# Moving one pool, one load, three weight jobs and some conversions in a fused attention and two-MLP kernel

## The chip, the cores and the metric

The kernel runs on one core of a Trainium2 chip. The metric is the device time of one execution in microseconds (us), the median of several runs; lower is better. Besides the timed runs there is one profiled execution, and every row shown below is from its trace. Engines are named as in the profile: PE (matmul), PEld (its weight loads), DVE (VectorE), ACT (ScalarE), POOL (GpSimd) and SP (SyncE). POOL and SP do little here but start DMA transfers.

## The reference, cut to what matters

Sparse attention, then two MLPs. The second MLP is where the change lies.

```python
def _moe_ref(x, w_in, w_out, s, b):            # first MLP, 512 -> 2048 -> 512
    r = np.maximum(x @ w_in, 0.0)
    return (s * (r * r) + b) @ w_out

def _moe2_ref(x, w_a, w_b, w_out):             # second MLP, 512 -> 1536 -> 512
    a = x @ w_a
    b = x @ w_b
    return (a * b @ w_out).astype(np.float32)

def reference(**kwargs):
    attn_out = _attn_ref(q, k, v)              # (4, 8, 576, 64), local and strided masks
    x = attn_out.transpose(0, 2, 1, 3).reshape(2304, 512)
    return _moe2_ref(_moe_ref(x, ...), ...)
```

## The kernel before

Every fp32 operand of a matmul is split into a high and a low part (ACT copies the high part, DVE subtracts to get the low one), and each product is three matmul passes.

**First MLP.** Five token blocks (`n` = 0 to 4), 16 feature tiles `f` each: products `h` and `acc`. Attention runs in between. The token blocks' inputs live in two rooms, `xp0` (16 KB per partition) and `xp1` (14 KB); the weights of this part live in `wpb`. In block `n == 4` the room `xp1` holds `spare`, which the weight jobs (below) use. Then these rooms are closed, and the pools `ws`, `tmp`, `rp`, `wx`, `gq`, `rq` are laid into the freed space from its start, in the order in which they are opened. A tile of a new pool waits until every use of the old tile under it has ended.

**Second MLP.** The 2304 tokens are three pairs of blocks of 384 tokens. Each pair has a gate part and an o part.
- The gate part has 12 groups `g`. A group is seven products of 6 matmuls (a 2 by 2 block scheme with seven products in place of eight), in this order: a11, s2, s3, s1, a12, a22 (`t4`, read from `wh`), s4. Text below writes (g, k) for the place right after product k of group g, k = 1 to 7. PSUM banks are reused inside a group: product 5 adds into the bank of product 1, so it waits until ACT has copied product 1 out (`quad` or `u`); product 6 adds into that of product 3; product 3 of the next group waits until DVE has read product 6 (`c`).
- Weights per group: two loads `wf<-w2s` of 512 KB (`s2`, `s3`, started two groups ahead by `fill`) and `wsrc<-w2d` of 256 KB (a11) and 128 KB (a22), started by `source` and then converted by ACT and DVE into `wf` and `wh` by `fill`. `wsrc` is one buffer: its next load is started when the conversion has read it and is needed after product 5 of the following group. All these, the x loads and the `o2w` loads go through the SP queue in order.
- The o part has 42 steps of 6 matmuls, step `i` with a 256 KB weight `o2w` from `w2o` (seven rooms, loaded seven steps ahead). Its right operands `gf` are made from `quad` by `g_form` (ACT, DVE, and in 18 of the 42 cases one more DVE operation on `quad`), 11 steps ahead. `o2_post` takes results out of PSUM.
- The next pair's input: `x2_load` brings `xr` (two blocks of 768 KB) from DRAM, `x2_bias` adds a bias (8 ACT steps in groups 9 to 11), and `x2_forms` has 18 steps (4 of them a DVE operation on `xr`, 14 an ACT copy and a DVE subtraction into `x2w`), done in the o part and the first group of the next pair.

**Weight jobs.** `sums(g, ...)` makes weight combinations once and writes them to DRAM through the POOL queue. Fifteen run in the last block of the first MLP, with `spare` as their room. The last one of these ends as the second MLP begins. The last three, `rest[0]` to `rest[2]`, run in the gate part of pair 0, one step at a time at places listed in `job_at`: one load step (two 256 KB loads `w2r`), 4 DVE sums, 4 ACT copies, 4 DVE subtractions, one step that writes 1792 KB to `w2o` (two pieces of 384 KB and four of 256 KB). Their rooms are `rings` 5, 11, 4 and 10.

**Order.** What runs on an engine is in program order as a scheduler laid it out when the kernel was built: it follows the order of the code where `in_order` holds a step behind the last matmul, and otherwise takes what its model finds ready. DVE and ACT have their own chains (`dve`, `act`) that keep the order of the code.

`o1_last` copies the last block of the first MLP out of PSUM: piece 0 and 3 into `hp` rooms, piece 1 into `hp`, piece 2 into `wx`. It runs between the last matmul of the first MLP and the first conversions of pair 0.

## Time and profile before

| | us |
|---|---|
| timed runs (3) | 907.13, 909.04, 909.31 (median 909.04) |
| profiled execution | 906.53 |
| its span, first to last instruction | 904.8 |
| PE busy in the span | 879.9 (97%) |
| DVE busy | 680.7 (75%) |
| ACT busy | 405.6 (45%) |

The profiled execution took 906.53 us, 1.7 us of them outside its span. It lies 0.6 us under the fastest timed run. PE is the engine that is nearly always busy; what is not PE time is 24.9 us of the span, 5.1 us of it in the first 100 us and 6.1 us in the last 55 us.

### The profile page before, as it was taken

To read this page: it belongs to the slowest core of one execution; us is meant where nothing else is said; L and a number is where in the kernel's file an instruction comes from. 1 tells how busy PE (TensorE), PEld (TensorE's weight loads), DVE (VectorE), ACT (ScalarE), POOL (GpSimd) and SP (SyncE) were. 2 spreads that over 40 slices of the span, in tenths; PEclk is the share of its full clock that TensorE was granted. 3 is DMA by queue.
4 is the path that set the end of the run, shared out by engine and by line. 5 is a ranking of instruction groups with operands and counts; after the bars stand their busy time and mean duration, and the time that the engine had idled before them with its cause. 6 is when DMAs were issued, how large, how long until landed. Compare 5 with 4: busy or idle time off the path is not lost.

```text
span 904.8 us, 17302 instructions
## 1 busy us (share of the span) xinstructions
PE 879.9 (97%) x6274; PEld 805.6 (89%) x6274; DVE 680.7 (75%) x1412; ACT 405.6 (45%) x879; POOL 145.6 (16%) x290
## 2 busy tenths in 40 slices
PE   8999999999999999999997999999999999999997
PEld 6778889999888899988886989999999999999997
DVE  6898995776766687637775888697777796877794
ACT  6777764333433343357563333363323462322251
POOL 6000000000000010014543121005300005200013
PEclk9999999999999999999998999999999999999999
DMA  9965534657766666458999688888667788666486
GB/s 233 289 198 170 158 73 138 156 147 163 199 172 171 163 189 170 125 161 307 365 329 323 205 323 279 301 270 260 182 200 249 251 274 250 187 206 202 163 266 186
DMA packets 184644, 195.70 MB, mean 216 GB/s; under 512 B 108272, under 2 KB 137712, under 8 KB 184560
## 3 DMA queue, kind: packets, MB, share of 16 engines
q1 hardware_dynamic: 166160, 147.07, 55.0%
q0 software_dynamic: 15520, 46.81, 14.8%
q10 hardware_dynamic: 2880, 0.72, 0.5%
q8 instruction: 50, 0.82, 0.4%
q14 instruction: 34, 0.28, 0.1%
HBM read 152.08 MB, written 42.47 MB: 215 GB/s over the span
## 4 chain that ended last, share of the span: by engine, by line
PE 69%; DMA 11%; DVE 6%; ACT 5%; issue 4%; POOL 2%; SPq 2%; POOLq 0%; ACTq 0%; DVEq 0%
PE pp L99 21%; PE h L99 16%; PE acc L99 14%; PE o L99 12%; DMA wsrc<-w2d 4%; DMA w2s<-w2t 2%; PE po L99 2%; DMA o2w<-w2o 1%; DVE quad L618 1%; PE pss L99 1%; DMA w2s<-spare 1%; PE ppt L102 1%; SPq L284 1%; DVE w2t L877 1%; DMA fqk<-in_k_dram 1%
## 5 line engine op out<-in xcount | busy, mean ns | idle before, releaser
L99 PE MATMUL pp<-x2w,wf 128*128 128x384 f32 x1296 | 235.4, 337 | 9.8 <-ACT quad L613 6.3
L99 PEld LDWEIGHTS pp<-x2w,wf 128*128 128x128 f32 x1296 | 227.3, 190 | 12.5 <-ACT quad L613 6.6
L99 PE MATMUL h<-x,w 128*128 128x512 f32 (+1 forms) x960 | 217.3, 374 | 1.1 <-ACT r L795 1.0
L99 PE MATMUL acc<-gt,w 128*128 128x512 f32 (+2 forms) x960 | 210.9, 368 | 1.0 <-ACT w L122 1.0
L99 PEld LDWEIGHTS acc<-gt,w 128*128 128x128 f32 x960 | 175.4, 188 | 24.3 <-ACT w L122 1.4
L99 PEld LDWEIGHTS h<-x,w 128*128 128x128 f32 x960 | 171.7, 188 | 25.7 <-ACT r L795 1.1
L99 PE MATMUL o<-gf,o2w 128*128 128x384 f32 x756 | 133.6, 337 | 2.8 <-issue 1.6
L99 PEld LDWEIGHTS o<-gf,o2w 128*128 128x128 f32 x756 | 131.2, 188 | 4.8 <-issue 4.6
L613 ACT ACTIVATE gf<-quad 128x384 fp32r<-128x384 f32 x126 | 64.1, 522 | 93.3 <-DVE quad L618 69.5
L795 ACT ACTIVATE r<-h 128x512 f32<-128x512 f32 (+1 forms) x80 | 44.2, 553 | 123.9 <-PE h L99 115.1
L1288 POOL DMA_DIRECT2D out_dram<-ot x92 | 51.5, 567 | 280.7 <-DVE ot L1274 274.9
L805 DVE TENSOR_TENSOR r<-r 128x384 f32<-128x384 f32 (+1 forms) x48 | 28.9, 602 | 60.1 <-ACT gt L802 60.0
L618 DVE TENSOR_TENSOR gf<-quad,gf 128x384 fp32r<-128x384 f32 x126 | 67.3, 548 | 7.0 <-ACT gf L613 5.2
L618 DVE TENSOR_TENSOR quad<-pp,quad 128x384 f32<-128x384 f32 x108 | 59.7, 552 | 7.8 <-PE pp L99 6.6
L853 POOL DMA_DIRECT2D w2d<-w2s x36 | 19.7, 546 | 207.8 <-DVE w2s L157 191.0
L613 ACT ACTIVATE wf<-wsrc 128x512 fp32r<-128x512 f32 x36 | 22.6, 628 | 66.2 <-PE pp L99 38.1
L141 ACT ACTIVATE raw<-raw 128x512 f32<-128x512 f32 x66 | 42.6, 669 | 8.1 <-DMA raw<-in_moe_w_a_dram 7.8
L147 DVE SCALAR_TENSOR_TENSOR raw<-raw 128x512 uint32<-128x512 uint32 x66 | 44.3, 687 | 0.7
L99 PE MATMUL pp<-x2w,wh 128*128 128x384 f32 x216 | 44.0, 338 | 0.4 <-DVE quad L618 0.3
L613 ACT ACTIVATE quad<-pp 128x384 f32<-128x384 f32 x36 | 17.5, 487 | 58.4 <-PE pp L99 58.3
L618 DVE TENSOR_TENSOR wf<-wsrc,wf 128x512 fp32r<-128x512 f32 x36 | 24.9, 692 | 21.6 <-ACT wf L613 21.6
L618 DVE TENSOR_TENSOR quad<-quad 128x384 f32<-128x384 f32 x72 | 39.8, 553 | 1.3
(175 smaller groups left out, 1005.1 us busy)
## 6 DMA issues: line engine op xcount, KB each, us to landing
wf<-w2s SPq DMA_DIRECT2D x72, 512.0 KB
o2w<-w2o SPq DMA_DIRECT2D x126, 256.0 KB
raw<-in_moe_w_out_dram SPq DMA_DIRECT2D x28, 512.0 KB
w2d<-w2s POOLq DMA_DIRECT2D x36, 256.0 KB, 3.7
w2r<-w2d POOLq DMA_DIRECT2D x36, 256.0 KB, 4.6
wsrc<-w2d SPq DMA_DIRECT2D x36, 256.0 KB
raw<-in_moe_w_in_dram SPq DMA_DIRECT2D x16, 512.0 KB
raw<-in_moe_w_a_dram SPq DMA_DIRECT2D x12, 512.0 KB
```

What stands on the lines that cost most here:

```text
L99: last_pe[:] = [nc.tensor.matmul(*args, **kwargs).ins]
L102: last_pe[:] = [nc.tensor.transpose(*args).ins]
L141: nc.scalar.activation(out=high.bitcast(F32), in_=high.bitcast(F32), func=AF.Copy, scale=HIGH_SCALE)
L147: nc.vector.scalar_tensor_tensor(out=low, in0=high, scalar=3, in1=low, op0=ALU.logical_shift_left, op1=ALU.bitwise_or)
L284: nc.sync.dma_start(out=room[p0:p0 + STR, first_:first_ + (z - a) // STR], in_=at[e])
L613: i = nc.scalar.activation(**kwargs).ins
L618: i = getattr(nc.vector, method)(**kwargs).ins
L795: relu = nc.scalar.activation(out=r, in_=ph, func=AF.Relu)
L805: nc.vector.tensor_tensor(out=r, in0=r, in1=r, op=ALU.mult)
L853: nc.gpsimd.dma_start(out=w2d[i - 1], in_=w)
L877: vector(out=out_, in0=in0, in1=in1, op=op)
L1288: engines[k % len(engines)].dma_start(out=at.rearrange("(j t) c -> t j c", t=STR), in_=st[i * STR:(i + 1) * STR, j:j + m].rearrange("t j a ...
```

## The change

Four edits, all in the second MLP.
- The pool `wx` is opened first, not fourth, so its one room lies at the start of the freed space (over `xp0`) instead of 28 KB into it (over the end of `xp1`). `ws` and `tmp` shift by 2 KB and stay over `xp0`; the first room of `rp` (ring 3) now touches `xp1`.
- `x2_load` brings one block per call. For the next pair, block one is called after product 2 of group 6, block two after product 2 of group 7; before, both came after product 2 of group 8. The x of pair 0 is loaded as before.
- The places of `rest[1]` and `rest[2]` in `job_at` change; those of `rest[0]` are the same, written differently. `rest[1]`: sums from group 3/4 to 2/3, copies from (5, 1..4) to (4, 3..6), subtractions from (5, 4..7) to (4, 6), (4, 7), (5, 1), (5, 2). `rest[2]`: sums from (7, 1..4) to (5, 4), (6, 5..7), copies from (8, 4..7) to (7, 1..4), subtractions from (9, 1..4) to (7, 5), (7, 7), (8, 5), (8, 6).
- In the o part of pairs 0 and 1 the x forms move from steps 0, 2, 5, 8, ..., 38 (14 calls) to 0, 14, 16, ..., 40 (15 calls), and the two 512 KB fills of group 1 of the next pair from steps 14 and 32 to 35 and 37.

```diff
-    def x2_load(pair):
-        xr = p2.tile([P, 2, KD, TB2], F32, tag="xr", name="xr")
-        for i in range(2):
-            c0 = (2 * pair + i) * TB2
-            queue_sp(out=xr[:, i], in_=o1[:, c0:c0 + TB2].rearrange("(k p) t -> p k t", p=P))
+    def x2_load(pair, xr=None):
+        i = 0 if xr is None else 1
+        xr = p2.tile([P, 2, KD, TB2], F32, tag="xr", name="xr") if xr is None else xr
+        c0 = (2 * pair + i) * TB2
+        queue_sp(out=xr[:, i], in_=o1[:, c0:c0 + TB2].rearrange("(k p) t -> p k t", p=P))
...
-    ws, tmp, rp, wx, gq, rq = (
-        pool(*i) for i in (("ws", 2), ("tmp", 6), ("rp", 5), ("wx", 1), ("gq", NQ2), ("rq", 4))
+    wx, ws, tmp, rp, gq, rq = (
+        pool(*i) for i in (("wx", 1), ("ws", 2), ("tmp", 6), ("rp", 5), ("gq", NQ2), ("rq", 4))
...
-        ((2, 1), (3, 5), (3, 6), (3, 7), (4, 7), *((5, k) for k in (1, 2, 3, 4))),
...
+            (1, 7), (2, 5), (2, 6), (2, 7), (3, 7), (4, 3), (4, 4), (4, 5),
+            (4, 6), (4, 6), (4, 7), (5, 1), (5, 2), (5, 3),
...
-    for k in (4, 5, 6, 7, 7):
-        job_at.setdefault((5, k), []).append(rest[1])
...
-            if pair + 1 < NP2 and g == 8:
+            if pair + 1 < NP2 and g == 6:
                 xr = in_order(x2_load, pair + 1)
+            if pair + 1 < NP2 and g == 7:
+                xr = in_order(x2_load, pair + 1, xr)
                 later_x += [x2_bias(xr), x2_forms(xr)]
...
-                if i == 0 or i % 3 == 2 and i < 40:
+                if i == 0 or i % 2 == 0 and i > 2 * NQ2:
                     next(later_x[1])
-                if i in (14, 32):
-                    in_order(fill, "s2" if i == 14 else "s3", (pair + 1) * NG2 + 1)
+                if i in (len(order2) - NW, len(order2) - NW + 2):
+                    in_order(fill, "s2" if i == len(order2) - NW else "s3", (pair + 1) * NG2 + 1)
```

PE's instructions keep their order throughout. On ACT, at the start of the gate part of pair 0, `spare<-w2t` is the last early weight job's copy, `o1s<-acc,sb` are pieces 0 and 2 of `o1_last`, `wh<-wsrc` is the first a22 conversion and `quad<-pp` the copy of product 1 (and, second, of product 5):

```order
 L888 ACTIVATE spare<-w2t 128x1024
-L613 ACTIVATE o1s<-acc,sb 128x512
-L888 ACTIVATE spare<-w2t 128x1024
-L613 ACTIVATE o1s<-acc,sb 128x512
-L613 ACTIVATE wh<-wsrc 128x256
-L613 ACTIVATE quad<-pp 128x384 x2
+L613 ACTIVATE o1s<-acc,sb 128x512 x2
+L613 ACTIVATE wh<-wsrc 128x256
+L613 ACTIVATE quad<-pp 128x384
+L888 ACTIVATE spare<-w2t 128x1024
+L613 ACTIVATE quad<-pp 128x384
```

The second `o1s`, `wh` and the first `quad` have moved ahead of the last `spare`.

On SP, in groups 6 to 8 of the gate part of pair 0 (pair 1 has the same piece): `xr` is the next pair's x, `w2s_152` to `w2s_154` are the weights of groups 8 to 10, `wsrc` those of a11 (128x512) and a22 (128x256):

```order
 L119 DMA wsrc<-w2d_130 128x256
+L119 DMA xr<-o_107 128x4x384
 L119 DMA wf<-w2s_152 128x1024 x2
 L119 DMA wsrc<-w2d_133 128x512
 L119 DMA wsrc<-w2d_135 128x256
+L119 DMA xr<-o_107 128x4x384
 L119 DMA wf<-w2s_153 128x1024 x2
 L119 DMA wsrc<-w2d_138 128x512
 L119 DMA wsrc<-w2d_136 128x256
-L119 DMA xr<-o_107 128x4x384 x2
 L119 DMA wf<-w2s_154 128x1024 x2
```

One block of x now stands in each of two groups, where two blocks stood in a row.

On DVE, in the o part of pair 0, up to the `o2_post` of the second form (`u2`), before and then now; `gf` and `quad` are the next operands, `xr` and `x2w` the x forms:

```order
L618 TENSOR_TENSOR xr_6666<-xr_6666 128x768
L618 TENSOR_TENSOR gf_6041<-quad_6191,gf_6041 128x384
L618 TENSOR_TENSOR quad_6191<-quad_6191 128x384
L618 TENSOR_TENSOR gf_6042<-quad_6351,gf_6042 128x384
L618 TENSOR_TENSOR quad_6351<-quad_6351 128x384
L618 TENSOR_TENSOR gf_6043<-quad_6505,gf_6043 128x384
L618 TENSOR_TENSOR quad_6505<-quad_6505 128x384
L618 TENSOR_TENSOR x2w_5468<-xr_6666,x2w_5468 128x384
L618 TENSOR_TENSOR gf_6044<-quad_6645,gf_6044 128x384
L618 TENSOR_TENSOR quad_6645<-quad_6645 128x384
L618 TENSOR_TENSOR u2_7026<-o2_6962,u2_7026 128x384
```

```order
L618 TENSOR_TENSOR gf_6041<-quad_6195,gf_6041 128x384
L618 TENSOR_TENSOR quad_6195<-quad_6195 128x384
L618 TENSOR_TENSOR gf_6042<-quad_6352,gf_6042 128x384
L618 TENSOR_TENSOR quad_6352<-quad_6352 128x384
L618 TENSOR_TENSOR gf_6043<-quad_6507,gf_6043 128x384
L618 TENSOR_TENSOR quad_6507<-quad_6507 128x384
L618 TENSOR_TENSOR gf_6044<-quad_6654,gf_6044 128x384
L618 TENSOR_TENSOR quad_6654<-quad_6654 128x384
L618 TENSOR_TENSOR u2_7022<-o2_6962,u2_7022 128x384
L618 TENSOR_TENSOR u2_7024<-o2_6963,u2_7024 128x384
L618 TENSOR_TENSOR gf_6045<-quad_6799,gf_6045 128x384
L618 TENSOR_TENSOR quad_6799<-quad_6799 128x384
```

Four x-form operations (three into `x2w`, one on `xr`) that stood between the start of the o part and `u2` now stand behind it; one on `xr` (of step 0) is still ahead of it.

## Rows read from the trace of the kernel before

**Rows 1.** What PE waited for: us in total, times, longest.
```profile
PE pp L99 <- ACT quad L613: 6.3, 1, 6.3
...
PE o L99 <- issue: 1.6, 2, 0.9
```

**Rows 2.** By stage: length, engines' busy us, PEclk, DMA share, GB/s; gate, o alternate.
```profile
587.27:632.97 45.70, 44.34 (x254) 43.76 (x253) 39.73 (x79) 20.92 (x45) 13.09 (x24) 1.00 0.85 268
632.97:721.20 88.23, 87.96 (x505) 87.14 (x504) 67.11 (x132) 29.28 (x64) 8.93 (x17) 1.00 0.67 217
721.20:767.30 46.10, 44.76 (x254) 43.84 (x254) 39.73 (x79) 21.77 (x47) 11.34 (x21) 1.00 0.85 271
767.30:854.70 87.40, 87.40 (x506) 87.40 (x506) 66.15 (x130) 24.47 (x54) 6.66 (x12) 1.00 0.59 192
...
484.63:587.27 102.64, 92.72 (x505) 90.03 (x504) 77.08 (x157) 35.53 (x76) 17.42 (x25) 0.95 0.80 280
```

**Rows 3.** PE's timeline, gate part of pair 0: start, us, instructions [idle before, releaser].
```profile
484.63 4.35 PE L99 MATMUL pp<-x2w,wf 128*128 128x384 f32 x24
495.31 2.29 PE L99 MATMUL pp<-x2w,wf 128*128 128x384 f32 x6 [6.33 <-ACT quad L613]
...
498.87 6.42 PE L99 MATMUL pp<-x2w,wf 128*128 128x384 f32 x36
...
520.76 3.29 PE L99 MATMUL pp<-x2w,wf 128*128 128x384 f32 x18
...
530.60 6.53 PE L99 MATMUL pp<-x2w,wf 128*128 128x384 f32 x36 [0.20 <-DVE quad L618]
...
568.02 3.29 PE L99 MATMUL pp<-x2w,wf 128*128 128x384 f32 x18
573.09 4.98 PE L99 MATMUL pp<-x2w,wf 128*128 128x384 f32 x18 [1.78 <-DVE c L618]
```

**Rows 4.** ACT's timeline at the start of that part, same columns.
```profile
486.99 1.06 ACT L888 ACTIVATE spare<-w2t 128x1024 fp32r<-128x1024 f32 x1 [2.83 <-DVE w2t L877]
493.88 0.69 ACT L613 ACTIVATE o1s<-acc,sb 128x512 f32<-128x512 f32 x1 [5.83 <-DMA w2s<-spare]
```

**Rows 5.** The chain that ended last, from 470 to 640: start, us, what.
```profile
515.67 8.16 DMA wsrc<-w2d
...
562.41 8.70 DMA wsrc<-w2d
...
624.11 6.54 DMA o2w<-w2o
```

**Rows 6.** SP's timeline: the load of x for pair 1.
```profile
556.01 0.97 SPq L119 DMA_DIRECT2D xr<-o  x2
```

**Rows 7.** By short stretches, columns of rows 2.
```profile
492.40:499.70 7.30, 4.39 (x17) 4.39 (x18) 3.08 (x6) 2.69 (x6) 0.00 (x0) 0.59 0.64 233
...
561.50:568.80 7.30, 7.30 (x44) 7.30 (x43) 6.14 (x12) 2.55 (x7) 3.79 (x6) 1.00 1.04 403
568.80:579.70 10.90, 9.12 (x44) 8.79 (x43) 7.00 (x14) 4.56 (x10) 0.00 (x0) 0.84 0.76 286
...
440.00:480.00 40.00, 40.00 (x178) 33.14 (x177) 28.77 (x53) 24.52 (x41) 17.17 (x28) 1.00 0.98 354
```

**Rows 8.** DVE's timeline: the weight job's 1024-column subtraction, and the o part of pair 0.
```profile
488.08 1.23 DVE L891 TENSOR_TENSOR w2t<-w2t,spare 128x1024 fp32r<-128x1024 f32 x1 [1.13 <-ACT spare L888]
...
592.27 0.95 DVE L618 TENSOR_TENSOR xr<-xr 128x768 f32<-128x768 f32 x1
...
597.86 0.55 DVE L618 TENSOR_TENSOR x2w<-xr,x2w 128x384 fp32r<-128x384 f32 x1
...
606.48 1.01 DVE L618 TENSOR_TENSOR u<-o,u 128x384 f32<-128x384 f32 x2
```

**Rows 9.** PE's timeline: the o parts of pairs 0 and 2.
```profile
607.13 23.21 PE L99 MATMUL o<-gf,o2w 128*128 128x384 f32 x132 [0.91 <-issue]
...
854.65 44.36 PE L99 MATMUL o<-gf,o2w 128*128 128x384 f32 x252
```

More of the change, by code (lines that the diff above doesn't have):

```diff
@@ L1127, in sparse_attention_two_mlps @@
             spare = p2.tile([P, 2 * DM], F32R, tag="z", name="spare")
-            xr = x2_load(0)
+            xr = x2_load(0, x2_load(0))
             ahead = [x2_bias(xr), x2_forms(xr)]
@@ L1339, in sparse_attention_two_mlps @@
     for job, at in zip(rest, (
-        (*((1, k) for k in (1, 2, 3, 4)), *((2, k) for k in (4, 5, 6, 7)), *((3, k) for k in (1, 2, 3, 4, 5))),
-        ((2, 1), (3, 5), (3, 6), (3, 7), (4, 7), *((5, k) for k in (1, 2, 3, 4))),
-        ((4, 1), *((7, k) for k in (1, 2, 3, 4)), *((8, k) for k in (4, 5, 6, 7)), *((9, k) for k in (1, 2, 3, 4, 5))),
+        (
+            (1, 1), (1, 2), (1, 3), (1, 4), (2, 4), (2, 5), (2, 6), (2, 7),
+            (3, 1), (3, 2), (3, 3), (3, 4), (3, 5),
+        ),
+        (
+            (1, 7), (2, 5), (2, 6), (2, 7), (3, 7), (4, 3), (4, 4), (4, 5),
+            (4, 6), (4, 6), (4, 7), (5, 1), (5, 2), (5, 3),
+        ),
+        (
+            (4, 1), (5, 4), (6, 5), (6, 6), (6, 7), (7, 1), (7, 2), (7, 3),
+            (7, 4), (7, 5), (7, 7), (8, 5), (8, 6), (8, 7),
+        ),
     )):
```

## Prediction

> **What bounds the kernel now.** I read the waits of PE first, then the time by stage, then PE's timeline where a stage is too long, and then the chain of waits and the timelines of ACT, SP and DVE at those places. PE is the bound: its one long wait in the second MLP is 6.3 us on an ACT copy, and 1.6 us in the o parts have no releaser that the profile names [rows 1]. The stages are the better measure. Three gate parts do the same 504 matmuls: that of pair 2 takes 87.40 us with PE busy all through, that of pair 1 88.23, that of pair 0 102.64 [rows 2]. So 15.2 us lie in the gate part of pair 0 and 0.8 in that of pair 1. The o parts of pairs 0 and 1 take 45.70 and 46.10 us [rows 2], where the same 252 matmuls of pair 2 take 44.36 [rows 9]: 1.3 and 1.7 us more. Everything the change can win is in these 19.1 us. PE's instructions and their order don't change, so the time can only move by waits, and by the clock that follows them.
>
> PE's timeline of pair 0 [rows 3] gives three losses. An undisturbed run of 36 matmuls takes 6.24 us from start to start (0.173 each), 6 take 1.04.
> - After product 4 of group 0, PE waits 6.33 us, and then needs 3.56 us for 12 matmuls (495.31 to 498.87) where 2.08 would do. The granted clock in that stretch averages 0.59 [rows 7], so part of it ran at 1.2 and not 2.4 GHz, after the wait. Together 6.33 + 1.48 = 7.8 us.
> - From 520.76 to 530.60 stand 42 matmuls, 7.28 us of work in 9.84: 2.6 us (groups 3 and 4).
> - At 568.02, 18 matmuls (3.12 us) should be followed by the next at 571.14; it starts at 573.09, and those 18 take 4.98 where the former took 3.29, at a granted clock of 0.84 [rows 3, 7]. 1.95 + 1.69 = 3.6 us (group 10).
> The rest, 1.2 us, is in small waits.
>
> **The copy-out room.** On ACT, the second `o1s` waits 5.83 us for a `w2s<-spare` transfer and starts at 493.88 [rows 4]. That is piece 2 of the copy-out, into `wx`, which lay over `xp1`, where the last early weight jobs have their room `spare`. `wh` and the first `quad` are queued behind it on ACT, product 5 waits for `quad`, and SP's next weight loads wait behind the store of that piece. Over `xp0`, whose last reader is a matmul that is over before, the wait is gone. It passes on to the first use of ring 3, a `gf` of group 2, more than 15 us later than those transfers start; nothing is left to wait for there. What is late next: DVE's 1024-column subtraction of the last job, 1.23 us [rows 8], no longer lies in the wait; it comes between the two DVE additions that free the bank of product 6, and I count 0.3 us for it (0 if PE has slack there, 1.2 at most). SP's store, its 128 KB of `wsrc` and two 512 KB fills now overlap the jobs' last writes, but they are needed only in groups 1 and 2, 5 us and more after they are started. Gain 7.8 - 0.3 = 7.5 us; bounds 6.6 and 7.8.
>
> **The x load in halves.** The loss in group 10 comes from `wsrc`: started at 562.41, landed 8.70 us later at 571.11 [rows 5], and PE went on 1.98 us after that, through ACT's and DVE's halves of the conversion and `c`. PE could have gone on at 571.14, so the load had to land by 569.16. On SP's queue ahead of it stands x, started at 556.01 [rows 6]. From there to the landing SP's queue moved 1536 KB of x, 1024 KB of fills and 256 KB of `wsrc`, 2.88 MB in 15.1 us: 191 GB/s, while POOL wrote `w2o` beside it. With one block the same stretch is 2048 KB, 2.10 MB, 11.0 us at that rate, and it has 13.15 us (556.01 to 569.16). So it lands 2.1 us early even with POOL writing all through: gain 3.6 us; bounds 0 (the rate falls under 160 GB/s) and 3.6. In pair 1 no weight job runs beside it, and the whole 0.8 us that its gate part has over that of pair 2 follows the same double load; gain 0.8, bounds 0 and 0.8.
>
> **The weight jobs.** Same steps, same bytes, earlier. `rest[0]` keeps its places, and with them the `w2o` writes beside `wsrc`, started at 515.67 and 8.16 us on its way [rows 5]: most of the 2.6 us in groups 3 and 4 stay. What leaves is DVE work: three of the sums of `rest[1]`, which stood beside the four subtractions of `rest[0]` in group 3. I take 0.5 us, bounds -0.5 and 2.6. Against it stands that all of it is packed closer. From the first `w2o` write in group 2 to the end of group 8 there will be 6.2 groups of 7.28 us, 45 us, with 1408 KB of weights in each, three times 1792 KB of `w2o`, 512 KB of job loads, 1536 KB of x and 256 KB of store: 16.8 MB, 372 GB/s. The traces show 354 GB/s over 40 us and 403 GB/s over 7.3 us [rows 7]. At 365 GB/s (between them, my choice) the excess is 0.8 us, at 354 2.3 us, at 403 none. Most of it can lag on POOL's side, where nobody waits; I take 1.0 us lost, bounds 0 and 3.6 (one such stall as in group 10). The `gf` rooms that `rest[1]` fills at (4, 3) were given to `rest[0]`'s writes some nine products before, about 9 us, so no copy waits there.
>
> The Trainium skill (DMA: Bandwidth & Descriptors, Specifications) puts HBM's limit per core at about 358 GB/s, which speaks against the packing: by that the 16.8 MB would take 46.9 us, 1.8 us more than the groups last. The row of 403 GB/s over 7.3 us is above it, so I don't take it as a ceiling; the sum does without it.
>
> **The o part.** DVE is the late engine at its start. The `u` additions that free the second pair of banks start at 606.48 [rows 8], though the matmuls they read ended at step 12, about 12.5 us into the part, near 600; step 18, which overwrites those banks, follows at 607.13 after 0.91 us of idle [rows 9]. Ahead of `u` stood four x-form operations now moved behind: three of 0.55 and one of 0.95 [rows 8], started 0.47 and 0.87 after one another, 2.3 us. `u` then ends 2.3 us earlier, and step 18 needs 1 us: the stall goes in both parts. From step 13 on, DVE has 0.5 us of `gf` per 1.04 us step, a form of 0.5 to 0.9 every second step and 6 us of `o2_post` in 30 us, under its limit, so nothing is late next. The last wait is `o2w`, landed 6.54 us after its start [rows 5], just behind the 512 KB fill of step 32. Now the fills come after the last `o2w` load, and have a whole group until they are used. Measured against the o part of pair 2, which has neither, the losses are 1.3 and 1.7 us; the end of that part differs a little, so I take 3.2 us for both, bounds 1.8 (only the waits without releaser, with their latency) and 4.0.
>
> **Sum.** 7.5 + 3.6 + 0.8 + 0.5 - 1.0 + 3.2 = 14.6 us. Against the profiled execution's 906.53: 891.9. The timed runs lie 0.6 to 2.8 us above that execution; with the middle, 1.7, the median should be 893.6.
>
> **Rivals.**
> - *Transfers take it back.* Between groups 3 and 8 some `wsrc` still land late. For it: 372 GB/s wanted, and a load that was 8.16 us under way beside only one job's writes. Against: the 2.1 us of margin in the worst group. Two stalls like that of group 10 cost 2 x 3.6 in place of the 1.0 that I count, 6.2 more: 899.8.
> - *Everything unhindered.* All 19.1 us but 0.3 go: 906.53 - 18.8 + 1.7 = 889.4, or 888.3 where the run lies only 0.6 above.
> - *The room doesn't do it.* Product 5 waits as long for another thing, the a22 `wsrc` behind the store and the jobs' last writes. Against: 5 us of time for 128 KB. A wait of half the length with its clock costs 3.2 + 1.5 = 4.7: 898.3.
> - *Slower.* SP's queue gets too little beside POOL's writes in all of groups 2 to 8, since the jobs now run nearly without a gap; in a group with a block of x that is decided at 160 GB/s, in one without at less. Then the seven `wsrc` loads started there each cost 3.6 us, 25.5 in all, where the gate part loses 15.2 - 7.5 = 7.7 beside the room. With the other gains, 7.5 + 0.8 + 3.2 = 11.5, the time is 906.53 + 17.8 - 11.5 + 1.7 = 914.5. Against: 191 GB/s in the worst stretch of the trace.
>
> **How the numbers follow.** The forecast has a chance of 0.62 with a range of its own of 890 to 897; the first rival 0.17, the unhindered case 0.09, the room 0.05, slower 0.04, and 0.03 for a result near no change, of small pieces of all. The predicted time is 893.5. The range takes in 888.0 and 900.0, with the two nearer rivals and the bounds of the unknown terms. 0.3%, 2.7 us, is about what a measurement of this kernel can tell from no change. Faster by more 0.93, within it 0.03, slower by more 0.04.
>
> **What would show it.** Right: in the gate part of pair 0 no wait of PE on an ACT `quad` and a clock of 1.00 in group 0; the gate part of pair 0 near 91 us and that of pair 1 near 87.4; no wait over 1 us on `c` in groups 9 to 11; o parts under 44.8 us, with `u` about 2 us earlier in them. Wrong: a stretch of clock below 1.00 in groups 2 to 9, ACT waits on `wsrc` over 5 us there, or a new PE wait on `wh` or `wf` in group 1. The stall of groups 3 and 4 should still be there, a little shorter; if it is gone, DVE was its cause and not the transfer.

## The result and the profile after

| | before | after |
|---|---|---|
| median of the timed runs | 909.75 us (907.13 to 911.74, 6 runs) | 895.83 us (895.18 to 897.73, 6 runs) |
| profiled execution, its span | 906.53 us, 904.8 us | 897.02 us, 895.3 us |
| after / before | | 0.985, interval 0.983 to 0.987 |

The kernel is 13.9 us faster by the medians and 9.5 us by the two profiled executions: that of before lay 3.2 us under its median, that of after 1.2 us over. The forecast was 893.5 us with 888 to 900 as the range. The total is 2.3 us off. The way to it was less good: in the gate part of pair 0 far less was won than was forecast.

By stage, profile of after, columns as in [rows 2]: gate part and o part of pair 0, of pair 1, gate part of pair 2, and its o part with the end of the kernel.

```profile
484.37:581.29 96.92, 91.15 (x506) 86.84 (x505) 77.56 (x157) 35.96 (x77) 18.16 (x26) 1.00 0.85 299
581.29:625.13 43.84, 43.84 (x254) 43.84 (x254) 40.09 (x80) 21.77 (x46) 13.04 (x24) 1.00 0.87 272
625.13:712.55 87.42, 87.33 (x504) 87.01 (x504) 66.56 (x130) 29.51 (x64) 9.05 (x17) 1.00 0.68 224
712.55:756.40 43.85, 43.85 (x254) 43.85 (x253) 40.36 (x81) 21.91 (x47) 10.74 (x19) 1.00 0.86 272
756.40:843.90 87.50, 87.50 (x507) 87.50 (x506) 65.59 (x129) 24.07 (x53) 7.34 (x13) 1.00 0.61 197
843.90:895.30 51.40, 44.54 (x254) 43.75 (x252) 34.29 (x68) 17.30 (x35) 11.51 (x20) 0.96 0.71 210
```

Against [rows 2] the gate part of pair 0 is 5.7 us shorter (102.64 to 96.92; forecast about 91) and the o parts 1.9 and 2.2 us (forecast 3.2 in all, measured 4.1). The limits of the later stretches, here and in [rows 2], lie up to 0.3 us beside the matmuls that they stand for. Counted between the starts of the matmuls, the gate part of pair 1 goes from 88.29 us (632.97 to 721.26) to 87.72 (625.13 to 712.85), 0.6 us shorter (forecast 0.8), and the last stretch from 50.15 to 51.25 us, 1.1 longer. The gate part of pair 0 begins 0.3 us earlier. These make the 9.5 us of the two profiles.

What PE waited for, profile of after (us in total, times, longest):

```profile
PE pp L99 <- DVE quad L618: 3.6, 7, 1.0
...
PE pp L99 <- DVE c L618: 1.9, 2, 1.4
```

The one wait of 6.3 us on an ACT copy [rows 1] is gone. In its place stand nine small ones on DVE. Where they are, PE's timeline of after shows (start, us, instructions, idle before and releaser):

```profile
484.37 5.37 PE L99 MATMUL pp<-x2w,wf 128*128 128x384 f32 x30
490.70 1.31 PE L99 MATMUL pp<-x2w,wh 128*128 128x384 f32 x6 [0.96 <-DVE quad L618]
...
499.13 3.29 PE L99 MATMUL pp<-x2w,wf 128*128 128x384 f32 x18
502.90 3.75 PE L99 MATMUL pp<-x2w,wf 128*128 128x384 f32 x18 [0.48 <-DVE c L618]
...
508.94 6.51 PE L99 MATMUL pp<-x2w,wf 128*128 128x384 f32 x36 [0.85 <-DVE quad L618]
...
516.33 3.28 PE L99 MATMUL pp<-x2w,wf 128*128 128x384 f32 x18
520.99 3.75 PE L99 MATMUL pp<-x2w,wf 128*128 128x384 f32 x18 [1.38 <-DVE c L618]
...
557.18 3.42 PE L99 MATMUL pp<-x2w,wf 128*128 128x384 f32 x18 [0.20 <-DVE quad L618]
561.32 3.49 PE L99 MATMUL pp<-x2w,wf 128*128 128x384 f32 x18 [0.72 <-DVE quad L618]
...
884.81 4.57 PE L99 MATMUL o<-gf,o2w 128*128 128x384 f32 x24 [0.94 <-DMA o2w<-w2o]
```

Counted from start to start against 0.173 us for each matmul, the gate part of pair 0 loses 1.2 us in group 0, 2.5 us in group 2, 3.4 us in groups 4 and 5 and 2.3 us in groups 8 and 9: 9.5 us with what is left. Before, the same count gave 8.0 in group 0, 2.7 in groups 3 and 4, 3.65 in group 10. So group 0 and group 10 are mended; groups 2 and 9 are new.

What the new ones have in common, the chain that ended last in after shows (start, us, what):

```profile
493.51 7.43 DMA wsrc<-w2d
...
510.70 8.31 DMA wsrc<-w2d
...
550.53 8.23 DMA wsrc<-w2d
```

Each of the three losses follows a `wsrc` that was 7.4 to 8.3 us on its way, as the two before did [rows 5]. SP's timeline of after at the first:

```profile
484.84 2.75 SPq L119 DMA_DIRECT2D o<-o1s  x3
...
488.72 4.68 SPq L119 DMA_DIRECT2D wf<-w2s  x2
493.51 1.42 SPq L119 DMA_DIRECT2D wsrc<-w2d  x2
```

Two 512 KB fills (`wf<-w2s`) go out ahead of the `wsrc` on the same queue, right after the stores of `o1s`, while POOL's writes of the last early job run. ACT's timeline of after shows who waits for it:

```profile
484.14 1.25 ACT L613 ACTIVATE o1s<-acc,sb 128x512 f32<-128x512 f32 x2
...
501.02 0.63 ACT L613 ACTIVATE wf<-wsrc 128x512 fp32r<-128x512 f32 x1 [6.39 <-DMA wsrc<-w2d]
...
519.12 0.63 ACT L613 ACTIVATE wf<-wsrc 128x512 fp32r<-128x512 f32 x1 [7.30 <-DMA wsrc<-w2d]
```

`o1s` no longer waits (in [rows 4] it did, 5.83 us); the conversion of `wsrc` does, 6.39 and 7.30 us, and PE's `c` and `quad` are behind it on ACT and DVE. Before had such waits too (6.21 us at 522.46, 7.16 at 571.22); the one ahead of group 2 is new.

### The profile page after: what moved, and what is told of

It reads as the page before. It is cut to its first block, busy times and chain, and to the rows that moved or that the text cites. A ratio compares the mean times of both kernels' runs of the same rounds, so it can differ in the third digit from the quotient of the medians.

```text
span 895.3 us, 17307 instructions
## 1 busy us (share of the span) xinstructions
PE 877.2 (98%) x6274; PEld 802.8 (90%) x6274; DVE 680.5 (76%) x1412; ACT 406.6 (45%) x879; POOL 146.1 (16%) x290
## 4 chain that ended last, share of the span: by engine, by line
PE 73%; DMA 8%; DVE 6%; ACT 5%; issue 4%; POOL 1%; SPq 1%; ACTq 0%; POOLq 0%; DVEq 0%
PE pp L99 22%; PE h L99 16%; PE acc L99 15%; PE o L99 14%; DMA wsrc<-w2d 4%; DMA w2s<-w2t 2%; PE po L99 2%; PE pss L99 1%; SPq L284 1%; PE ppt L102 1%; DVE w2t L877 1%; ACT spare L888 1%; PE fpo L99 1%; DVE quad L618 1%; DVE gt L123 1%
## 5 line engine op out<-in xcount | busy, mean ns | idle before, releaser
L99 PE MATMUL pp<-x2w,wf 128*128 128x384 f32 x1296 | 232.9, 335 | 4.1 <-DVE quad L618 2.0
L99 PEld LDWEIGHTS pp<-x2w,wf 128*128 128x128 f32 x1296 | 224.8, 188 | 7.2 <-DVE quad L618 3.7
L99 PEld LDWEIGHTS pp<-x2w,wh 128*128 128x128 f32 x216 | 37.7, 188 | 3.4 <-DVE quad L618 3.0
```

The lines of the kernel that those rows point to most:

```text
L99: last_pe[:] = [nc.tensor.matmul(*args, **kwargs).ins]
```

## The experiments

The theory with which they began: each part of the change does what its own place in the trace says, and what is left in the gate part of pair 0 comes from `wsrc`, which stands on SP's queue behind fills while POOL writes. The rivals: the total of bytes in groups 2 to 8 is the limit; DVE's work for the jobs is; or waits are only handed on from one place to the next. Theories are numbered within each expectation. Medians are compared by the ratio to the kernel before on the same chip.

**Each part alone, on the kernel before.** The room:

```diff
-    ws, tmp, rp, wx, gq, rq = (
-        pool(*i) for i in (("ws", 2), ("tmp", 6), ("rp", 5), ("wx", 1), ("gq", NQ2), ("rq", 4))
+    wx, ws, tmp, rp, gq, rq = (
+        pool(*i) for i in (("wx", 1), ("ws", 2), ("tmp", 6), ("rp", 5), ("gq", NQ2), ("rq", 4))
```

> The kernel before with the pool wx opened first, and nothing else. Theory 1 (each edit removes its own stall): the 6.33 us wait on the ACT quad and its clock go, less about 1.2 us for DVE's 1024-column subtraction, 6.6 us gained, a ratio of 0.993. Theory 2 (the pause let transfers drain, and its loss is partly handed on to the wsrc loads of groups 1 and 2): the wait goes, but a new wait on c of 0.5 to 1 us and one on quad appear in groups 1 and 2, 2.5 us together, so 4 us gained, a ratio of 0.9955; the stall of group 10 (1.95 us and its clock) stays in both.

Measured: 906.24 us, ratio 0.996 (0.9946 to 0.9973), 3.6 us. PE's timeline of this kernel:

```profile
487.18 5.39 PE L99 MATMUL pp<-x2w,wf 128*128 128x384 f32 x30
493.55 1.34 PE L99 MATMUL pp<-x2w,wh 128*128 128x384 f32 x6 [0.97 <-DVE quad L618]
...
508.96 1.32 PE L99 MATMUL pp<-x2w,wh 128*128 128x384 f32 x6
511.15 6.51 PE L99 MATMUL pp<-x2w,wf 128*128 128x384 f32 x36 [0.87 <-DVE quad L618]
...
565.85 3.28 PE L99 MATMUL pp<-x2w,wf 128*128 128x384 f32 x18
573.00 5.87 PE L99 MATMUL pp<-x2w,wf 128*128 128x384 f32 x18 [3.86 <-DVE c L618]
```

Group 0 loses 1.3 us in place of 8.0, so the wait itself is worth 6.7 us against before's profile. (It is worth up to 8 us against the profiles of the other kernels that keep the old room, where group 0 loses 9.1 to 9.3.) The loss after it, 1.9 us in group 2, is here too with nothing else changed: it comes with the room. And the stall of group 10 stays, in this execution larger than before (7.15 us from start to start in place of 5.07). The ratio is that of theory 2; theory 1's 0.993 lies outside the interval.

The x load in halves:

```diff
-            if pair + 1 < NP2 and g == 8:
+            if pair + 1 < NP2 and g == 6:
                 xr = in_order(x2_load, pair + 1)
+            if pair + 1 < NP2 and g == 7:
+                xr = in_order(x2_load, pair + 1, xr)
```

> The kernel before with x of the next pair loaded in two halves, after product 2 of groups 6 and 7, and nothing else. Theory 1: the stall of group 10 (3.6 us with its clock) and the 0.8 us of pair 1 go, 4.4 us, a ratio of 0.995; the 6.33 us wait in group 0 stays. Theory 2: the stall of group 10 comes from the last job's writes as much as from x; about half of it stays (2 us, as in the kernel after), and the gain is 2 to 3 us, a ratio of 0.997.

Measured: 904.68 us, ratio 0.9952 (0.9933 to 0.997), 4.4 us; forecast 3.6 + 0.8. PE's timeline of this kernel in group 10:

```profile
569.09 6.41 PE L99 MATMUL pp<-x2w,wf 128*128 128x384 f32 x36
...
576.90 6.51 PE L99 MATMUL pp<-x2w,wf 128*128 128x384 f32 x36 [0.20 <-DVE quad L618]
```

The 36 matmuls that were split by 1.78 us of idle [rows 3] run through; of 3.65 us 0.6 are left. Theory 1.

The places of the weight jobs, the same table as in the change (some lines of it):

```diff
-        ((2, 1), (3, 5), (3, 6), (3, 7), (4, 7), *((5, k) for k in (1, 2, 3, 4))),
...
+            (1, 7), (2, 5), (2, 6), (2, 7), (3, 7), (4, 3), (4, 4), (4, 5),
+            (4, 6), (4, 6), (4, 7), (5, 1), (5, 2), (5, 3),
```

> The kernel before with the places of the second and third remaining weight jobs moved, and nothing else. Theory 1 (fewer DVE steps beside one another): 0.5 us gained in groups 3 and 4, and a loss of 1 us at most elsewhere, ratio 0.999 to 1.001. Theory 2 (the jobs' writes then stand closer): the stall of groups 3 and 4 grows from 2.6 to above 3 us, and the third job's writes no longer stand beside x, so the stall of group 10 shrinks by 1 to 3 us; ratio 0.997 to 0.999.

Measured: 907.66 us over 12 runs, ratio 0.9972 (0.9956 to 0.9988), 2.5 us. The profiled execution (911.31 us) lies above its median and does not show the gain: groups 4 and 5 lose 2.2 us, group 10 3.7 us. The ratio is theory 2's, but neither of the two changes that it expected is in this profile. So the jobs alone bring something, but this run does not show where.

The o parts:

```diff
-                if i == 0 or i % 3 == 2 and i < 40:
+                if i == 0 or i % 2 == 0 and i > 2 * NQ2:
                     next(later_x[1])
-                if i in (14, 32):
-                    in_order(fill, "s2" if i == 14 else "s3", (pair + 1) * NG2 + 1)
+                if i in (len(order2) - NW, len(order2) - NW + 2):
+                    in_order(fill, "s2" if i == len(order2) - NW else "s3", (pair + 1) * NG2 + 1)
```

> The kernel before with the x forms and the two fills moved in the o parts, and nothing else. Both theories: 1.9 us gained in the first o part and 2.2 in the second, as the trace of the kernel after has them (43.84 and 43.85 us), 4.1 us, a ratio of 0.9955; the forecast was 3.2 us, 0.9965. No stage before the first o part changes by more than 0.5 us.

Measured: 905.45 us, ratio 0.9955 (0.9937 to 0.9973), 4.1 us. PE's timeline: the o part of pair 0 is one row without a wait, and takes 43.83 us from start to start.

```profile
589.09 44.00 PE L99 MATMUL o<-gf,o2w 128*128 128x384 f32 x252
632.92 5.36 PE L99 MATMUL pp<-x2w,wf 128*128 128x384 f32 x30
```

The four gains add up to 3.6 + 4.4 + 2.5 + 4.1 = 14.6 us, where all together give 13.6 (0.985 of 909.75), well within their intervals.

**Which half of the o part's edit does what.** On the kernel before, the x forms moved and the fills left at steps 14 and 32:

```diff
-                if i == 0 or i % 3 == 2 and i < 40:
+                if i == 0 or i % 2 == 0 and i > 2 * NQ2:
                     next(later_x[1])
```

> The kernel before with only the x forms moved in the o parts of pairs 0 and 1; the fills stay at steps 14 and 32. In the kernel before each of these parts loses about 1.1 us at step 18 and 0.8 to 0.9 at step 40, beside a few tenths after it. Theory 1 (DVE's u additions make the first, the 512 KB fill of step 32 the second): the first goes, the second stays, parts of 44.7 to 45.0 us. Theory 2 (DVE is late for both, or the fills are): parts of 43.8, or of 45.5 and more.

Measured: one run, 906.95 us. PE's timeline of this kernel:

```profile
588.75 23.12 PE L99 MATMUL o<-gf,o2w 128*128 128x384 f32 x132
612.18 21.46 PE L99 MATMUL o<-gf,o2w 128*128 128x384 f32 x120 [0.31 <-ACT x2w L613]
...
721.81 41.90 PE L99 MATMUL o<-gf,o2w 128*128 128x384 f32 x240
764.56 2.56 PE L99 MATMUL o<-gf,o2w 128*128 128x384 f32 x12 [0.85 <-DMA o2w<-w2o]
```

The wait at step 18 [rows 9] is gone in both o parts. The one on `o2w` at the end of the second stays, 0.85 us; with the fills moved as well it is gone (the run with the o parts alone). So the forms made the first loss, and the fills make the second: theory 1, with parts of 44.74 and 45.15 us. That it is the fill of step 32 and not that of step 14 is argued from its place alone. (One execution: the 0.31 us at 612.18 isn't explained by either.)

**The x load put back, on the kernel after.** `x2_load` brings both blocks again, in group 8:

```diff
-            if pair + 1 < NP2 and g == 6:
+            if pair + 1 < NP2 and g == 8:
                 xr = in_order(x2_load, pair + 1)
-            if pair + 1 < NP2 and g == 7:
-                xr = in_order(x2_load, pair + 1, xr)
```

> The kernel after with both blocks of x loaded after product 2 of group 8 again, and nothing else undone. Alone, on the kernel before, the halves gave 0.9952, 4.4 us. Theory 1 (the stall of group 10 needs both x and the third job's writes; with the jobs' new places only the last 384 KB of them stand beside x): 1 to 2.5 us lost, 0.8 of them in the gate part of pair 1, ratio 0.986 to 0.988. Theory 2 (x alone is enough, since the time per group is shorter now): the full 4.4 us are lost, ratio 0.990.

Measured: 898.84 us, ratio 0.9879 (0.9848 to 0.9911), 3.0 us over after's median. PE's timeline of this kernel:

```profile
563.69 3.28 PE L99 MATMUL pp<-x2w,wf 128*128 128x384 f32 x18
568.14 3.75 PE L99 MATMUL pp<-x2w,wf 128*128 128x384 f32 x18 [1.17 <-DVE c L618]
```

The stall of group 10 is back (2.7 us in all), though the jobs write only twice beside it, at 552.67 and 559.99, and the gate part of pair 1 is 88.49 us again. The gate part of pair 0 is only 0.8 us longer than after's in this profile (97.73), since groups 4 and 5 and groups 8 and 9 lose 2.2 us less. By the medians the halves are worth 3 us in this kernel. The ratio is theory 1's, but its interval reaches theory 2's 0.990 and overlaps after's.

**The jobs put back, on the kernel after** (the old table, in place of the new one):

```diff
-            (1, 7), (2, 5), (2, 6), (2, 7), (3, 7), (4, 3), (4, 4), (4, 5),
-            (4, 6), (4, 6), (4, 7), (5, 1), (5, 2), (5, 3),
...
+        ((2, 1), (3, 5), (3, 6), (3, 7), (4, 7), *((5, k) for k in (1, 2, 3, 4))),
```

> The kernel after with the places of the second and third remaining weight jobs as before, and nothing else undone. Alone, on the kernel before, the new places gave 0.9972. Theory 1 (they spread work and keep the third job's writes away from the loads of x): without them 1 to 3 us are lost, ratio 0.987 to 0.988, with the loss at groups 9 and 10. Theory 2 (with x in halves they only bring the second job's writes closer to the first): nothing lost or up to 1 us gained, ratio 0.984 to 0.985, with a smaller loss in groups 4 and 9.

Measured: 895.89 us, ratio 0.9859 (0.9834 to 0.9884): no difference from after. In its profiled execution the gate part of pair 0 takes 94.84 us, 2.1 less than after's, with 2.9 us lost in groups 4 and 5, 1.0 in groups 6 to 9 and nothing in group 10. With the x load in halves the new places bring nothing that can be measured (theory 2).

**The writes of the jobs taken away, on the kernel after.** The `w2o` writes of the last three jobs don't run in the gate part; the rows that they would fill get other values in the first MLP:

```diff
-        for e in range(2):
+        for e in range(0 if g >= NG2 + NQ2 - 3 else 2):
...
+                if 8 <= i < 29:
+                    nc.gpsimd.dma_start(
+                        out=w2o[3 + (i - 8) // 7][:, (i - 8) % 7], in_=w.rearrange("p (e c) -> p e c", e=2)
+                    )
```

> The kernel after, with the w2o writes of the last three weight jobs left out of the gate part of pair 0; their rows of w2o get other values in the first MLP instead, so the output is not the reference's. All ACT and DVE steps of the jobs stay. Theory 1 (wsrc is late because POOL's writes share the transfers): wsrc takes 5 us or less in groups 3 to 9, the losses of groups 4 and 9 (3.4 and 2.3 us) go, that of group 2 (2.5 us, beside the last early job's writes) stays; the gate part of pair 0 is about 91 us. Theory 3 (the jobs' ACT and DVE steps make the stalls): the losses of groups 4 and 9 stay above 2 us each, the gate part above 95 us.

Measured: one run, 907.99 us; the early writes delay the start of the gate part to 497.21, so only its length can be compared: 93.86 us in place of 96.92. PE's timeline of this kernel:

```profile
512.02 3.29 PE L99 MATMUL pp<-x2w,wf 128*128 128x384 f32 x18
516.48 3.77 PE L99 MATMUL pp<-x2w,wf 128*128 128x384 f32 x18 [1.17 <-DVE c L618]
...
522.52 6.51 PE L99 MATMUL pp<-x2w,wf 128*128 128x384 f32 x36 [0.87 <-DVE quad L618]
```

Groups 4 and 5 lose 0.7 us in place of 3.4, groups 8 and 9 1.2 in place of 2.3, while DVE's work for the jobs is all there (77.70 us busy, 77.56 in after). The `wsrc` of group 4, 8.31 us on its way in after, is read 5.7 us after its start (524.28 to 529.98). So it is POOL's writes that slow `wsrc` there, not DVE: theory 1, though half of the loss of groups 8 and 9 stays and the stage comes to 93.9 us, not to about 91. Group 2 loses 3.2 us, no less than in after, behind a `wsrc` of 8.12 us: none of the writes that were taken away run so early.

**`wsrc` ahead of the fill, on the kernel after.** The same loads, but the two `source` calls (a11 of three groups on, a22 of two groups on) go out ahead of the 512 KB fill `s3` and not behind it:

```diff
-            if i:
-                in_order(source, "a22", i + 1)
...
             in_order(fill, "a22", i + 1)
+            in_order(source, "a11", i + 3)
+            in_order(source, "a22", i + 2)
...
                 in_order(fill, "s3", i + 2)
-            in_order(source, "a11", i + 3)
```

> The kernel after, with one change of order on SP's queue: in every group both wsrc loads of the next group are started right after the a22 conversion that frees the buffer, ahead of the 512 KB s3 fill, instead of behind it. No byte and no operation of another engine changes. Theory 1 (the stalls left in the gate part of pair 0 come from wsrc landing late because it queues behind the s3 fill while POOL writes): wsrc lands some 3 us earlier, its 7.4 to 8.3 us in flight in groups 2, 3 and 8 fall to 5 or less, the losses of groups 2, 4 and 9 (2.5, 3.4 and 2.3 us) go, and the gate part of pair 0 falls from 96.9 to about 90 us: ratio to the kernel before near 0.977. Theory 2 (the rate of all transfers is the limit, 16.8 MB in six groups): the s3 fills become late in place of wsrc, and the gate part stays above 95 us: ratio 0.984 to 0.986. Theory 3 (DVE's own order in these groups makes the stalls): no change, 0.985.

Measured: 893.32 us (892.62 to 895.44, 5 runs), ratio 0.9829 (0.9805 to 0.9853). The stretch of the gate part of pair 0, columns of [rows 2]:

```profile
485.28:577.09 91.81, 89.42 (x505) 87.05 (x504) 77.34 (x157) 36.18 (x77) 18.11 (x26) 1.00 0.89 312
```

PE's timeline of it, groups 2 to 4:

```profile
500.70 6.40 PE L99 MATMUL pp<-x2w,wf 128*128 128x384 f32 x36
...
508.54 6.53 PE L99 MATMUL pp<-x2w,wf 128*128 128x384 f32 x36 [0.40 <-DVE quad L618]
...
515.95 6.40 PE L99 MATMUL pp<-x2w,wf 128*128 128x384 f32 x36
```

And ACT's timeline, the conversion in group 4 that waited 7.30 us for a DMA in after:

```profile
515.15 0.63 ACT L613 ACTIVATE wf<-wsrc 128x512 fp32r<-128x512 f32 x1 [3.71 <-PE pp L99]
```

The conversion now waits for PE and not for the load: started at 510.14, the load is read 5.0 us later, where in after it took 8.31. Groups 4 and 5 lose 0.5 us (3.4 in after), group 2 0.7 (2.5), groups 8 and 9 1.4 (2.3), and group 1, which lost next to nothing, 0.8.

So the order mends the load of group 4. It does not mend the other two, as the chain that ended last in this kernel shows:

```profile
492.85 7.69 DMA wsrc<-w2d
...
546.36 8.20 DMA wsrc<-w2d
```

In after these took 7.43 and 8.23 us. The first is started earlier here, 7.6 us after the start of the gate part and not 9.1; that PE loses less in group 2 comes with that, and a part of it has only moved to group 1.

Nearly the same bytes (28.6 MB by the row; after has 29.0) go at 312 GB/s where after had 299, in a stage 5.1 us shorter. So by this stage neither the total of bytes was the limit (theory 2) nor DVE's order, which is as it was (theory 3). Of theory 1 only a part held: it had all three loads at 5 us or less, a stage of about 90 us and a ratio of 0.977. By the medians the gain on after is 2.5 us, and the interval still takes in after's 0.985.

The new order may have a price. The second o part waits for its first `o2w`, which it does not in after:

```profile
708.96 44.14 PE L99 MATMUL o<-gf,o2w 128*128 128x384 f32 x252 [0.50 <-DMA o2w<-w2o]
```

The two kernels below with this order have the wait too (0.35 and 0.64 us), but so has the kernel without the writes (0.65), so its cause is open.

**The last early job's subtraction behind two additions, on the kernel after.** DVE's 1024-column step, 1.23 us, moves out of the way of PE's wait in group 0:

```diff
-                if j < EARLY:
+                if j < EARLY - 1:
                     for _ in added[j]:
                         pass
+                elif j == EARLY - 1:
+                    for _ in range(5):
+                        next(added[j])
...
             add(v_, pc, v_)
+            if i == 0:
+                with after(list(last_dve)):
+                    for _ in range(2):
+                        in_order(next, added[EARLY - 1], None)
```

> The kernel after, with DVE's 1024-column subtraction of the last early weight job placed behind the two DVE additions of group 0 that free the bank of product 6, and nothing else. Theory 1 (the 0.96 us wait of PE in group 0 is that one instruction in DVE's order): the wait goes, 1.1 us less in group 0, and the job's write starts about 1 us later. If the stall of group 2 is due to the transfers, it stays or grows a little (2.5 to 3 us): ratio 0.984. Theory 2 (product 6 waits for a load): the wait stays, ratio 0.985.

Measured: 896.61 us, ratio 0.9867 (0.984 to 0.9895): nothing gained on after. PE's timeline of it:

```profile
486.43 5.39 PE L99 MATMUL pp<-x2w,wf 128*128 128x384 f32 x30
491.66 1.20 PE L99 MATMUL pp<-x2w,wh 128*128 128x384 f32 x6
...
505.30 5.32 PE L99 MATMUL pp<-x2w,wf 128*128 128x384 f32 x18 [1.64 <-DVE c L618]
```

The wait of 0.96 us in group 0 is gone, as intended. PE then comes to group 2 the sooner, and waits there for the same `wsrc`: 1.64 us on `c`, where after had 0.48, and group 2 loses 3.8 us, more than the 2.5 to 3 that were expected. (The profiled execution took 902.12 us, 5.5 over its median, so the sizes in it are large.) Here a wait that was removed ahead of a later one on a late load was handed on.

**Combinations.** `wsrc` first, with the subtraction moved as well:

```diff
+            in_order(source, "a11", i + 3)
+            in_order(source, "a22", i + 2)
...
+                    for _ in range(2):
+                        in_order(next, added[EARLY - 1], None)
```

> Both earlier edits on the kernel after: the wsrc loads ahead of the s3 fill, and DVE's 1024-column subtraction of the last early job behind the two additions that free the bank of product 6. Theory 1 (in the run with the subtraction moved alone, its 1.2 us came back in group 2 only because wsrc was late there): with wsrc ahead of the fill it stays gained, the gate part of pair 0 is near 90.5 us, ratio 0.9815. Theory 2 (the gain is handed on whatever stands ahead on SP's queue): gate part 91.5 to 92.5, ratio 0.983.

Measured: 893.33 us, ratio 0.9816 (0.9788 to 0.9844). The gate part takes 92.58 us: group 0 loses nothing, but group 2 1.9 us and groups 8 and 9 2.5. The ratio is theory 1's and the stage theory 2's, so it stays open which holds; the kernel can't be told from `wsrc` first alone.

`wsrc` first, with the jobs at their old places:

```diff
+            in_order(source, "a11", i + 3)
+            in_order(source, "a22", i + 2)
...
+        ((2, 1), (3, 5), (3, 6), (3, 7), (4, 7), *((5, k) for k in (1, 2, 3, 4))),
```

> The kernel after with the wsrc loads ahead of the s3 fill, and the weight jobs at their places of before. If the new places bring nothing once x is in halves (0.9859 without them against 0.985 with them), this is the same as with the new places, 0.983, and the losses of groups 8 and 9 (1.4 us) shrink to below 1 us while those of group 4, where the second job's sums stand beside the first job's subtractions, come up to 1 us. If the new places matter once wsrc is in time, because DVE is then the late engine in group 3, it is 0.9845 or more.

Measured: 893.29 us, ratio 0.982 (0.9789 to 0.9851). The gate part takes 90.39 us, the shortest of all, with the loss in group 9 gone, 1.1 us left in group 2 and 1.0 in groups 6 and 7. In both combinations the load of group 2 is still slow, 7.89 and 7.29 us. By the medians the three are level at 893.3 us, 2.5 us under after's median. Their intervals overlap after's, and they were compared with it only through the kernel before. The simplest of them is the table of before with `wsrc` ahead of the fill.

## Why the prediction was right, and where it was not

**The room: mechanism right, size too large.** The ACT wait is gone and the clock in the gate part is 1.00 where [rows 7] had 0.59 after that wait; both were named as signs. Of the 7.8 us, 1.2 stay in group 0. The forecast counted 0.3 for the 1024-column subtraction, with 1.2 as the bound; the bound was right. DVE's timeline of after:

```profile
488.95 1.23 DVE L891 TENSOR_TENSOR w2t<-w2t,spare 128x1024 fp32r<-128x1024 f32 x1 [0.66 <-ACT spare L888]
490.10 1.21 DVE L618 TENSOR_TENSOR quad<-pp,quad 128x384 f32<-128x384 f32 x2
```

The subtraction starts just after DVE's other work has run out, and the two additions behind it free PE's bank: there was no slack. The step that failed is another: "they are needed only in groups 1 and 2, 5 us and more after they are started". It counts the store, 128 KB of `wsrc` and the two fills, and stops there. The load that comes late is the next one on the same queue, the `wsrc` at 493.51: it took 7.43 us, and 2.5 us are lost in group 2. The room alone gives 3.6 us where 7.5 were forecast. So the rival that the room doesn't do it was right in part: the wait did pass on to a `wsrc`, but two groups later and at a third of the size. That ring 3 would wait for nothing was right; the `gf` copies of group 2 are not late for their rooms in after.

What makes this one load slow is not shown. It took 7.3 to 7.9 us with one fill less ahead of it, and 8.12 us without the later writes of POOL. The writes of the last early job, which run beside it, were in every kernel with the new room. In before, where it was started 10.9 us after the last of them (489.61) and not 3.0, it was read 4.6 us after its start (500.54 to 505.15). That points at these writes, but more than this differs between the two.

**The x load: right.** 4.4 us alone, 3.0 us when put back, against 4.4 forecast for both pairs. The margin of 2.1 us was too good, though: 2.3 us are lost in groups 8 and 9 of after, behind a `wsrc` of 8.23 us that stands on SP's queue after half of x and two fills. A mean rate over 15 us of mixed traffic doesn't give the landing of one load in it.

**The jobs: no net effect, near the forecast of -0.5 (0.5 gained, 1.0 lost by packing), for another reason.** Putting the jobs back changes the median by 0.1 us. The loss of groups 3 and 4 was said to be a little shorter, since DVE work leaves. It was 3.4 us, not shorter, and the kernel with the jobs put back shows 2.9. The run without writes shows its cause: POOL's `w2o` writes. That the stall stays if the transfer is the cause was in the prediction, and held.

**The packing: from the wrong quantity, and not shown to be the wrong size.** 1.0 us was counted, from a total of bytes against a rate. In groups 4 to 9 of after 5.7 us are lost (3.4 + 2.3), where the forecast left 4.3 (2.6 - 0.5, the 1.0, and 1.2 in small waits). That is 1.4 us more, less than one profile of each kernel can size, and with the jobs at their old places the median is the same. What decides is when one load lands: the bytes stay the same when `wsrc` goes ahead of a fill, and groups 4 and 5 then lose 0.5 us in place of 3.4. The rival "transfers take it back" named the load and the sign; its 6.2 us were not reached. ACT waits of over 5 us on `wsrc` were named as a sign of being wrong, and they came (6.39 and 7.30 us). But before had one of 6.21 us at the same place already (at 522.46), so this sign could not tell.

The Trainium skill (DMA: Bandwidth & Descriptors, Queues, rings and completion order) says that each DMA engine takes one ring's descriptors in order and takes turns between the queues. That agrees with two runs on the load of group 4: it is read 5.0 us after its start with one fill fewer ahead of it on its own queue, and 5.7 us after it without the other queue's writes, where it took 8.31 in after. It leaves the loads of groups 2 and 9 open, which stayed at 7.69 and 8.20 us with the same change of order. The limit of about 358 GB/s that the Trainium skill gives for a core (DMA: Bandwidth & Descriptors, Specifications) did not hold in [rows 7], at 403 GB/s over 7.3 us.

**The o parts: mechanism right, size too small.** 4.1 us for 3.2. `u` came early enough: the `u` additions of the first o part stand at 598.20 in after, 16.9 us into it, where before they stood at 19.2 (606.48 from 587.27): 2.3 us earlier, as forecast. The step that failed is the yardstick, 44.36 us for the o part of pair 2 [rows 9]. That row runs to the end of its last matmul, where an undisturbed one has 44.00, and 43.84 to the next start, by which the stages were measured. So each part had 0.5 us more to give.

**Not seen: the end.** In after the last o part waits 0.94 us for `o2w` at 884.81, where before's profile had no such wait. It isn't the change's: the profiles of all twelve kernels of the experiments have it, at 0.2 to 1.0 us, those with one edit on the kernel before too (0.4 to 0.75), and none of the four edits moves a load there. What delays it, and why the one profile of before has none, is open.

**The sum.** Forecast 14.6; measured 13.6 by the ratio, interval 11.8 to 15.5. By the two profiles it is 9.5. Against the forecast the gate part of pair 0 gives 4.9 less (5.7 for 7.5 + 3.6 + 0.5 - 1.0 = 10.6): 0.9 in group 0, 2.6 in groups 1 and 2, 1.4 behind them. The o parts give 0.9 more, the gate part of pair 1 0.2 less, the end 1.1 less, and the earlier start 0.3 more.

The difference between 9.5 and 13.9 lies in which executions were profiled. The profiles of the four kernels that keep the old room show a part of it. PE's wait in group 0 is 7.2 to 7.4 us in them, not 6.33; the last o part waits for `o2w`; and in three of the four the gate part of pair 0 begins 1.5 to 3.1 us later than before's. One of them, the run with the o parts alone (PE's timeline):

```profile
498.08 2.29 PE L99 MATMUL pp<-x2w,wf 128*128 128x384 f32 x6 [7.24 <-ACT quad L613]
```

So before's profile was one of its faster executions, and the room is worth more than that profile shows. The forecast added 1.7 us to come from the profile to the median; in after the median lies 1.2 us under the profile. The gain between the profiles was forecast 5.1 us too large, and this allowance, 2.9 us too high, took back more than half of it. That the total is nearer than the terms were is luck.

## What to carry to other kernels

Before moving work to earlier places, look at what stands on the issuing queue ahead of the small load that is needed next: loads of 256 KB behind two 512 KB fills were 7 to 8 us on their way. Putting them ahead of one of the fills cut one of three such flights from 8.31 to 5.0 us; the stage was 5.1 us shorter in the profiles, the kernel 2.5 us by the medians. When a long wait is removed, search for the next load that the same engine needs and compare its time of flight in the trace, not its size, with the time that is left. Follow the queue past the loads that were on the list: here the late one was the next behind them. And take as "undisturbed" only a stretch whose matmuls run at their own pace from start to end.

## What the runs showed of the hardware

- Time of flight under load is far from what size says: `wsrc` loads of 128 and 256 KB took 4.0 to 10.6 us in the chains of these traces (4.03 in before, started at 548.67). The 10.59 us stand in the run with the room alone (started at 560.43), at the load behind both blocks of x and two fills.
- A stage can run faster with the same bytes and the same queues: 312 GB/s in place of 299 for the order of the `wsrc` loads, one profile each. The DMA share went from 0.85 to 0.89.
- The granted clock is a cost of its own behind a wait. After 3.86 us of idle in the run with the room alone, 18 matmuls took 5.87 us where 3.29 is usual, at a granted clock of 0.52 (573.00 to 578.70); after 1.64 us in the run with the subtraction moved, 5.32 us, at 0.67 (505.30 to 510.46). After 1.38 us in after they took 3.75 us at a granted clock of 1.00 (520.99 to 524.70), so those 0.5 us are not the clock's.
- The kernel's executions differ by some 3 us in places that look the same in the program, so one profile of each kernel sizes a term to 2 or 3 us at best.
